# Filler products and an earlier first output product behind the experts' weights, with the first piece of w_out loaded last and decoded in halves

## The chip, the cores and the metric

The kernel runs on one core of one Trainium2 chip. The metric is the device time of one execution in microseconds (us), given as the median of three runs. One further execution was recorded by the profiler; all rows below are of that one.

## The reference

Attention over a window of 128 positions, then a soft mixture of experts, then a feed-forward layer with a leaky ReLU. The change lies between the last two.

```python
def _moe_ref(x, phi, w1, w2):                 # x 2304x512, 8 experts of 4 slots
    logits = x @ phi
    d = softmax over tokens of logits
    slot_input = (d.T @ x).reshape(E, S_per_e, D)
    for e in range(E):
        h = np.maximum(slot_input[e] @ w1[e], 0.0)
        slot_out[e] = h @ w2[e]
    c = softmax over slots of logits
    return c @ slot_out

def _moe2_ref(x, w_in, w_out):                # w_in 512x2048, w_out 2048x512
    h = x @ w_in
    g = np.maximum(0.01 * h, h)
    return g @ w_out
```

## The kernel before, in words

The program is one stream of instructions per engine, written out by hand: parts of the work are put into a list with a number each, the list is sorted by that number, and the instructions are issued in that order. Engines wait for one another through semaphores; within an engine nothing overtakes.

**The experts.** After attention, the experts' weights (units of 1 MB, four experts' blocks of 128 x 512 each) are multiplied as they arrive: 16 units of w1, then 16 units of w2 (line 824, numbered `i` = 0 to 15 by `g * FC + fc`). The last ten units have no room earlier and are loaded by line 793, each into a slot `p0`, `p1`, ... All these loads go through SP's queue, in the order of the program. Ahead of the last four units (`PRE`) SP also issues the first pieces of the next layer's weights: `load_wi(0)` and `load_wo(0)`, 1 MB each. After the last unit ScalarE copies the sum out of PSUM (line 859), TensorE transposes it (`to_soT`, line 762), and VectorE copies it into `soT` (line 765).

**The feed-forward layer.** c @ slot_out @ w_in is computed as c @ (slot_out @ w_in), so that a piece of w_in (256 columns, `NCH` = 8 pieces) is first multiplied with the 32 slots: `emit_M(c, 0)` (line 882, four products of 32 rows each), a copy by ScalarE (line 885), `emit_M(c, 1)` (line 887, one product that adds the four), a rounded copy by ScalarE (line 889) and the rest of the rounding by VectorE (line 890). Then follow units of 384 tokens x 128 columns: `stage1` (line 910), two activations by ScalarE (`round_g` line 914, `full_g` line 918), their difference by VectorE (`rest_g`, line 922), and `emit_o`, the output product: nine products of 512 columns (line 931), three for each of three groups of 128 tokens. Every two units of columns need a new piece of w_in and w_out. Both `emit_M` parts and `stage1` write one of two PSUM buffers named `ph`, so each waits until ScalarE has read the buffer written two before.

**Decoding.** w_in and w_out lie in memory as 64-bit floats. `decode` (line 719) turns a piece into 32-bit ones: two ScalarE activations on halves of 512 columns, and on VectorE two TENSOR_SCALAR and four SCALAR_TENSOR_TENSOR; a piece of w_out is then also split into a rounded part (a CAST by ScalarE) and a rest (a TENSOR_TENSOR by VectorE), again in halves. Half 0 of piece 0 of w_out holds the columns that units 0 and 1 use, half 1 those of units 2 and 3.

**The order.** Unit `n` has the number `n` for `stage1`, and `n + ZO["O"]` = `n + 3.986` for `emit_o`. Pieces are decoded, and `emit_M` issued, at numbers worked out from `YD[c]`:

```python
o = n + (ZO["O"] if n >= ZO["r"] else ZO["O"] - (ZO["r"] - n) * ZO["d"])
at_(-2, emit_M, 0, 0)
at_(-1 + ZO["M1"], emit_M, 0, 1)
for c in range(1, NCH):
    at_(YD[c] + ZO["M"], emit_M, c, 0)
    at_(YD[c] + ZO["M"] + ZO["m"], emit_M, c, 1)
```

So four `stage1`, both parts of `emit_M` for piece 0 and both for piece 1 stand ahead of the first output product. `warm` (line 150), in the attention part, multiplies the identity with itself into a buffer that nobody reads; each call of `matmul` there makes two records in the trace, since 32-bit products take two passes.

Of the kernel before, what the change touches and what calls it, by code (L numbers as in the profile page):

```python
# [9 lines left out]
F32 = mybir.dt.float32  # L10
# [11 lines left out]
def attn_softmoe_ffn(ctx: ExitStack, tc: tile.TileContext, q, k, v, phi, w1, w2, w_in, w_out, cst_in, out):  # L22
# [96 lines left out]
    with tc.manual_schedule():  # L119
# [552 lines left out]
        FPC = NF // NCH  # L672
        fw = DFF // NCH
        TB = 384
        x0 = off["x0"]

        def parts(w, *os):
# [110 lines left out]
        while i < len(units_w):  # L788
            if i == len(units_w) - PRE:
                load_wi(0, "p12")  # L790
                load_wo(0, "p13")
            o, src = put_w(i, j, slot(f"p{k}")[:, 0:512 * (4 - j)])
            nc.sync.dma_start(out=o, in_=src)  # L793
            i, j, k = i + 1, 0, k + 1
        csts = [t.bitcast(F32R).rearrange("p (t a s) -> p t a s", t=5, a=4) for t in (view("xT", 640, 512), ar[:, x0 + 1536:x0 + 2176])]
        cg = []

# [18 lines left out]

        for b in range(2):
            csplit(b)
        for g in range(E // 4):
            p2 = ps.tile([128, DM], F32, tag="pb0", name="pb")  # L820
            for fc in range(FC):
                t = W.pop((1, g, fc, 0))
                for j in range(4):
                    nc.tensor.matmul(p2[32 * j:32 * j + 32, :], lhsT=hT[g][:, fc, :], rhs=t[j],
                                     start=(fc == 0), stop=(fc == FC - 1), tile_position=(0, 32 * j))
                i = g * FC + fc
                if i == HI:
                    to_hT(1)
                if i == SOI:
                    to_soT(0)  # L830
                if i == 6:
                    load_wi(1, "a3")
                    cctx.close()
                    pools["b"] = ctx.enter_context(tc.tile_pool(name="bp", bufs=1, side="right", reuse_waits="tile"))
                    alloc_wo(0, "b0", "b1")
                    d0 = decode(0, False)
                    for f in d0[0] + d0[1]:
                        f()
                    d0 = decode(0, True)
                    load_wo(1, "a2")  # L840
                    load_wi(2, "b2")
                if i == 9:
                    for f in d0[0] + d0[1]:
                        f()
                if i == 1:
                    cg.extend(slot(x, F32R) for x in ("p11", "p10"))
                    ctr(0)
                    csplit(2)
                if i == 2:
                    ctr(1)  # L850
                    csplit(3)
                if i in (4, 5):
                    ctr(i - 2)
            if g == E // 4 - 1:
                load_wo(2, "p9")
                load_wi(3, "p0")
                load_wo(3, "p12")
            so = ar[:, x0 + F:x0 + F + DM]
            nc.scalar.copy(out=so, in_=p2)
            if g == E // 4 - 1:  # L860
                for f in d0[2][::2]:
                    f()
        to_soT(1)
        for f in d0[2][1::2]:
            f()
        bctx.close()


# [5 lines left out]
        rings["g1"], rings["g2"] = [[[gx[:, TB * i:TB * i + TB] for i in range(4)], 0] for gx in (cg[1], G2)]  # L874

        Mq = {}

        def emit_M(c, part):
            p = psc.tile([128, 512], F32, tag="ph", name="ph")
# [77 lines left out]
        def at_(y, f, *a):  # L957
            ev.append((y, len(ev), lambda: f(*a)))

        for n, u in enumerate(units):  # L960
            o = n + (ZO["O"] if n >= ZO["r"] else ZO["O"] - (ZO["r"] - n) * ZO["d"])
            at_(n, stage1, *u)
            at_(n + ZO["T"], round_g, *u)
            at_(n + ZO["H"], full_g, *u)
            at_(n + ZO["V"], rest_g, *u)
            at_(o, emit_o, *u)
            if u[2] == NF - 1 or (u[0], u[2]) == (0, FH - 1):
                for i in range(3):
                    at_(o + (.01 * i if u[0] in (0, 1, NB - 1) else i), finish)
        YD = {c: per * (c - 1) if 2 * c <= NCH else per * (NCH // 2 - 1) + 2 + 7 * (c - NCH // 2) for c in range(1, NCH + 1)}  # L970
        at_(-2, emit_M, 0, 0)
        at_(-1 + ZO["M1"], emit_M, 0, 1)
        for c in range(1, NCH):
            at_(YD[c] + ZO["M"], emit_M, c, 0)
            at_(YD[c] + ZO["M"] + ZO["m"], emit_M, c, 1)

        def dec(c, split, y, y1):
            ops = []

            def go(l, i):  # L980
                ops.extend(decode(c, split) if not ops else [])
                ops[l][i]()
            for i in range(2):
                at_(y + ZO["q"] + .01 * i, go, 0, i)
            for i in range(6):
                at_(max(y + ZO["D"] + ZO["w"] * i, y1), go, 1, i)
            for i in range(4 if split else 0):
                at_(y + ZO["t"] + ZO["u"] * (i // 2), go, 2, i)
        for c in range(1, NCH):
            if c == 1:  # L990
                dec(1, False, YD[c] - 2, ZO["f"])
            dec(c, True, YD[c], ZO["g"] if c == 1 else -9)
            if c + 1 < NCH:
                dec(c + 1, False, YD[c + 1] - 2, -9)
        at_(-.9, load_wi, 4, "p13")
        at_(2.05, load_wo, 4, "a3")
        sl = ("a2", "b2", "p9", "p0", "p12", "p13")
# [54 lines left out]
```

## Time and profile before

| | us |
|---|---|
| median of the three runs | 460.52 |
| lowest and highest of the three | 457.16, 460.90 |
| the profiled execution | 457.5 |
| its span, first to last instruction | 455.7 |

The profiled execution lies 0.3 us above the lowest run and 3.0 us below the median. In the page and the views times count from the start of the span. PE is TensorE, PEld its weight loads, DVE is VectorE, ACT is ScalarE, SP the queue that issues the DMAs; PEclk or the granted clock is the share of TensorE's full clock. A record's duration includes the time in which a product drains; records of one engine overlap, so the pace of a series is read from the distance of the starts or from the chain, not from one record's duration.

### The profile page before, as it was taken

The numbers are of one execution on the slowest core, as the hardware profiler recorded it, in microseconds if no ns is written. First come the engines' busy times: TensorE is split into PE (matmuls) and PEld (weight loads), VectorE is DVE, ScalarE is ACT, GpSimd is POOL, SyncE is SP. The second block draws the span as 40 slices with busy tenths as digits, with TensorE's granted clock in tenths as the row PEclk, the third lists the DMA queues.
The fourth block names the chain that finished last, engine by engine and source line by source line (L and its number), as shares of the span: only waits on it lengthen the run. The fifth ranks groups of instructions, "written<-read, shape, count | busy, mean of one in ns | idle before, by whom it ended". The sixth has DMA issues, their size and how long they took to land.

```text
span 455.7 us, 9878 instructions
## 1 busy us (share of the span) xinstructions
PE 432.9 (95%) x3506; PEld 338.9 (74%) x3506; DVE 278.3 (61%) x891; ACT 242.3 (53%) x560; POOL 109.8 (24%) x288
## 2 busy tenths in 40 slices
PE   7899999999999989996699999999999999999996
PEld 6797887888788764341277787787888888888885
DVE  5999999999999833033799857756223225224221
ACT  5576776777677531240677665556345333333331
POOL 3476676667477523020000000000000000000000
PEclk9999999999999999998589999999999999999999
DMA  9339778668669899999997300000003003001001
GB/s 170 97 118 231 211 219 232 170 200 238 179 199 239 261 337 340 371 391 388 399 384 251 116 1 0 1 1 0 1 0 138 1 0 140 1 1 47 23 1 69
DMA packets 66593, 70.30 MB, mean 154 GB/s; under 512 B 23056, under 2 KB 41648, under 8 KB 66544
## 3 DMA queue, kind: packets, MB, share of 16 engines
q1 hardware_dynamic: 66544, 69.66, 48.3%
q8 instruction: 28, 0.46, 0.4%
q14 instruction: 21, 0.17, 0.1%
HBM read 64.85 MB, written 4.72 MB: 153 GB/s over the span
## 4 chain that ended last, share of the span: by engine, by line
PE 83%; DMA 5%; DVE 4%; ACT 3%; SPq 2%; issue 1%; POOL 1%; ACTq 0%; DVEq 0%; POOLq 0%
PE acc L931 44%; PE o_ps L389 7%; PE sm L295 5%; PE ph L910 4%; PE st L336 4%; PE st L337 3%; PE tp L255 3%; DMA p<-in_moe_w_dram 3%; PE pb L773 3%; SPq L793 2%; PE tp L430 2%; ACT kb L268 1%; DVE junk L305 1%; PE ph L882 1%; PE tp L456 1%
## 5 line engine op out<-in xcount | busy, mean ns | idle before, releaser
L931 PE MATMUL acc<-p,p 128*128 128x512 f32 x648 | 161.0, 393 | 0.0
L931 PEld LDWEIGHTS acc<-p,p 128*128 128x128 f32 x648 | 120.4, 188 | 25.8 <-issue 1.2
L922 DVE TENSOR_TENSOR p<-ar,p 128x384 fp32r<-128x384 f32 x96 | 53.5, 557 | 103.9 <-ACT ar L918 103.6
L914 ACT ACTIVATE p<-ph 128x384 fp32r<-128x384 f32 x96 | 47.2, 492 | 107.1 <-PE ph L910 107.1
L931 PE MATMUL acc<-b,p 128*128 128x512 f32 x216 | 56.1, 404 | 0.0
L305 DVE CUSTOM_DVE_ANT_0 junk<-sm,ar 128x256 bf16<-128x256 f32 (+2 forms) x160 | 53.6, 375 | 3.2 <-PE sm L295 2.8
L931 PEld LDWEIGHTS acc<-b,p 128*128 128x128 f32 x216 | 40.9, 192 | 9.9 <-issue 1.2
L918 ACT ACTIVATE ar<-ph 128x384 f32<-128x384 f32 x96 | 46.6, 486 | 0.0
L344 ACT ACTIVATE ar<-st 128x512 f32<-128x512 f32 x64 | 38.3, 598 | 14.8 <-PE st L337 9.3
L389 PE MATMUL o_ps<-ar 128*64 128x65 f32 x1024 | 40.2, 225 | 0.7 <-POOL ar L360 0.7
L389 PEld LDWEIGHTS o_ps<-ar 128*64 128x64 f32 x1024 | 36.0, 138 | 5.1 <-issue 1.5
L336 PE MATMUL st<-kq 128*128 128x256 f32 (+1 forms) x160 | 39.8, 278 | 0.0
L295 PE MATMUL sm<-kb,qb 96*128 96x256 f32 (+2 forms) x160 | 35.0, 312 | 4.3 <-ACT kb L268 1.9
L337 PE MATMUL st<-qb,kb 128*128 128x256 f32 (+1 forms) x160 | 35.6, 269 | 0.7 <-DMA qb<-ms 0.7
L910 PE MATMUL ph<-p,p 128*128 128x384 f32 x96 | 33.1, 346 | 1.8 <-DVE p L890 0.9
L268 ACT ACTIVATE qb<-tp 64x288 fp32r<-64x288 f32 x64 | 27.7, 432 | 9.3 <-PE tp L255 7.8
L273 DVE SCALAR_TENSOR_TENSOR kq<-tp,qb 64x288 fp32r<-64x288 f32 x64 | 29.2, 457 | 4.2 <-ACT qb L268 2.2
L268 ACT ACTIVATE kb<-tp 64x288 fp32r<-64x288 f32 x64 | 27.9, 436 | 6.2 <-PE tp L255 4.9
L275 DVE TENSOR_TENSOR kq<-tp,kb 64x288 fp32r<-64x288 f32 x64 | 29.1, 455 | 1.7
L281 POOL TENSOR_SCALAR_AFFINE_SELECT kq<-qb 64x576 fp32r<-64x576 f32 x32 | 21.3, 664 | 35.2 <-ACT qb L268 30.0
L336 PEld LDWEIGHTS st<-kq 128*128 128x128 f32 (+1 forms) x160 | 28.6, 179 | 1.4 <-issue 0.9
L337 PEld LDWEIGHTS st<-qb,kb 128*128 128x128 f32 (+1 forms) x160 | 28.6, 179 | 0.9 <-DMA qb<-ms 0.9
(164 smaller groups left out, 575.7 us busy)
## 6 DMA issues: line engine op xcount, KB each, us to landing
p<-in_moe_w_dram SPq DMA_DIRECT2D x56, 256.0 KB
p<-in_moe_w_dram SPq DMA_DIRECT2D x9, 1024.0 KB
p<-in_moe_w_in_dram SPq DMA_DIRECT2D x5, 1024.0 KB
p<-in_moe_w_out_dram SPq DMA_DIRECT2D x5, 1024.0 KB
ar<-in_k_dram SPq DMA_DIRECT2D x32, 144.0 KB
ar<-in_q_dram SPq DMA_DIRECT2D x32, 144.0 KB
out_dram<-ar SPq DMA_DIRECT2D x18, 256.0 KB
ar<-in_v_dram SPq DMA_DIRECT2D x32, 128.0 KB
```

What stands on the lines that cost most here:

```text
L268: nc.scalar.activation(out=b1, in_=pr, func=AF.Copy, scale=2.0 ** (g % H - 2) if half else 1.0)
L295: nc.tensor.matmul(sl, lhsT=Q1[0:MROW, 128 * t:128 * t + mr], rhs=K1[0:MROW, c0:c1], start=True, stop=True)
L305: nc.vector.tensor_tensor_reduce(out=jk[0:mr, 0:n], in0=sl, in1=maskt[0:mr, m0:m0 + n], op0=ALU.add, op1=ALU.max, accum_out=mn[g % 2][0:mr ...
L336: nc.tensor.matmul(sl, lhsT=KX[:, k0:k1], rhs=QA[:, q0:q1], start=True, stop=False)
L337: nc.tensor.matmul(sl, lhsT=kb[g % R][:, k0:k1], rhs=qb[g % R][:, q0:q1], start=False, stop=True)
L344: nc.scalar.activation(out=e, in_=sts.pop((g, s)), func=AF.Exp, scale=2.0 ** -(g % H + 1))
L389: nc.tensor.matmul(o_ps[64 * u:64 * u + 64, t, :], lhsT=lt, rhs=r, start=st, stop=sp, tile_position=(0, 64 * u))
L910: nc.tensor.matmul(p, lhsT=mst[:, 128 * f:128 * f + 128], rhs=rhs, start=True, stop=True)
L914: nc.scalar.activation(out=G[t0, f][0], in_=H1[t0, f], func=AF.Prelu, alpha=0.01)
L918: nc.scalar.activation(out=gg, in_=H1.pop((t0, f)), func=AF.Prelu, alpha=0.01)
L922: nc.vector.tensor_tensor(out=g2, in0=G0.pop((t0, f)), in1=g1.bitcast(F32), op=ALU.subtract)
L931: nc.tensor.matmul(acc[t0][t], lhsT=(g1, g1, g2)[k][:, 128 * t:128 * t + 128], rhs=(WO1, WO2, WO1)[k][c][:, i], start=((f == 0 or (j, f) = ...
```

## The change

The load of piece 0 of w_out moves from ahead of the last four expert units to behind them. Its decoding, which was written into the experts' loop, moves into the list and is issued in halves, by numbers written out in a table `FIRST`, as are the decodings of piece 1. `keep` multiplies the identity with itself: 2, 8 and 8 times ahead of expert units 13, 14 and 15, then 4, 3, 3, 4 and 5 times between the steps that lead to the first output product (table `WX`). The last copy out of PSUM is shared by ScalarE and VectorE. Output products are issued closer to their `stage1` at first (`n + 1.9`, growing by 0.13 a unit up to the old distance), and `emit_M` for piece 1 behind the second output product.

```diff
+        WX = {13: 2, 14: 8, 15: 8, "s": 4, "t": 3, "m": 3, "b": 4, "h": 5}
...
             if i == len(units_w) - PRE:
                 load_wi(0, "p12")
-                load_wo(0, "p13")
...
             i, j, k = i + 1, 0, k + 1
+        load_wo(0, "p13")
...
+        wps = ps.tile([128, 128], F32, tag="w", name="w", bufs=1)
+
+        def keep(n, t):
+            for i in range(n):
+                nc.tensor.matmul(t[:, 0:128], lhsT=ident, rhs=ident, start=True, stop=True)
+
         for g in range(E // 4):
             p2 = ps.tile([128, DM], F32, tag="pb0", name="pb")
             for fc in range(FC):
                 t = W.pop((1, g, fc, 0))
+                keep(WX.get(g * FC + fc, 0), wps)
...
                     d0 = decode(0, False)
                     for f in d0[0] + d0[1]:
                         f()
-                    d0 = decode(0, True)
                     load_wo(1, "a2")
                     load_wi(2, "b2")
-                if i == 9:
-                    for f in d0[0] + d0[1]:
-                        f()
...
             so = ar[:, x0 + F:x0 + F + DM]
-            nc.scalar.copy(out=so, in_=p2)
             if g == E // 4 - 1:
-                for f in d0[2][::2]:
-                    f()
+                nc.scalar.copy(out=so[:, 0:256], in_=p2[:, 0:256])
+                nc.vector.tensor_copy(so[:, 256:512], p2[:, 256:512])
+                keep(WX["s"], wps)
+            else:
+                nc.scalar.copy(out=so, in_=p2)
         to_soT(1)
-        for f in d0[2][1::2]:
-            f()
+        keep(WX["t"], wps)
...
+        wpc = psc.tile([128, DM], F32, tag="acc5", name="acc", bufs=1)
...
-            o = n + (ZO["O"] if n >= ZO["r"] else ZO["O"] - (ZO["r"] - n) * ZO["d"])
-            at_(n, stage1, *u)
+            o = n + min(1.9 + .13 * n, ZO["O"])
+            y = n + (.2 if n >= 4 else 0)
+            at_(y, stage1, *u)
...
         at_(-2, emit_M, 0, 0)
+        at_(-1.9, keep, WX["m"], wpc)
         at_(-1 + ZO["M1"], emit_M, 0, 1)
-        for c in range(1, NCH):
+        at_(-.9, keep, WX["b"], wpc)
+        at_(1.05, keep, WX["h"], wpc)
+        at_(3.05, emit_M, 1, 0)
+        at_(3.5, emit_M, 1, 1)
+        for c in range(2, NCH):
...
+        FIRST = {(0, True): ((-2.5, -1.5), (-2.4, -.95, -2.3, -.94, -2.2, .38), (-.93, -.92, 1.18, 1.38)),
...
+        dec(0, True, 0, 0)
...
-                dec(c + 1, False, YD[c + 1] - 2, -9)
+                dec(c + 1, False, YD[c + 1] - 2, 3.5 if c == 1 else -9)
```

In SP's queue, where the last expert units and the first pieces are issued, stands before:

```order
L692 DMA p_3538<-in_moe_w_in_dram 128x4x512
L697 DMA p_3540<-in_moe_w_out_dram 128x2x1024
L793 DMA p_3542<-in_moe_w_dram 128x4x512
L793 DMA p_3544<-in_moe_w_dram 128x4x512
L793 DMA p_3546<-in_moe_w_dram 128x4x512
L793 DMA p_3548<-in_moe_w_dram 128x4x512
```

and now, with `load_wi` and `load_wo` one line further down in the file:

```order
L693 DMA p_3538<-in_moe_w_in_dram 128x4x512
L793 DMA p_3540<-in_moe_w_dram 128x4x512
L793 DMA p_3542<-in_moe_w_dram 128x4x512
L793 DMA p_3544<-in_moe_w_dram 128x4x512
L793 DMA p_3546<-in_moe_w_dram 128x4x512
L698 DMA p_3548<-in_moe_w_out_dram 128x2x1024
```

The four expert units move up by one load, and the piece of w_out stands behind them; all that follows keeps its place.

On TensorE, from expert unit 14 (before) and the fillers ahead of unit 15 (now) to the first output product (`pb` is the experts' sum, `w` and `acc` on the left of `ident` are what the fillers write, `ph` the shared buffer, `acc<-b` an output product), stands before:

```order
L824 MATMUL pb<-p_3546,ar 32x512 x4
L824 MATMUL pb<-p_3548,ar 32x512 x4
L762 MATMUL pa<-ident,ar 128x128 x4
L882 MATMUL ph<-ar 32x256 x4
L887 MATMUL ph<-ar,blk 128x256
L910 MATMUL ph<-p_3567,p_3749 128x384 x2
L882 MATMUL ph<-ar 32x256 x4
L910 MATMUL ph<-p_3567,p_3749 128x384
L887 MATMUL ph<-ar,blk 128x256
L910 MATMUL ph<-p_3567,p_3749 128x384
L931 MATMUL acc<-b_3657,p_3568 128x512 x3
```

and now, where line 824 is the filler and 832 the experts' product:

```order
L824 MATMUL w<-ident 128x128 x8
L832 MATMUL pb<-p_3546,ar 32x512 x4
L824 MATMUL w<-ident 128x128 x4
L763 MATMUL pa<-ident,ar 128x128 x4
L824 MATMUL w<-ident 128x128 x3
L888 MATMUL ph<-ar 32x256 x4
L824 MATMUL acc<-ident 128x128 x3
L893 MATMUL ph<-ar,blk 128x256
L824 MATMUL acc<-ident 128x128 x4
L916 MATMUL ph<-p_3568,p_3764 128x384 x2
L824 MATMUL acc<-ident 128x128 x5
L937 MATMUL acc<-b_3658,p_3569 128x512 x3
```

The second `emit_M` (both parts) and two of the four `stage1` have left the place ahead of the first output product, and 19 fillers stand there. Where they went, behind the first output product, is this:

```order
L916 MATMUL ph<-p_3568,p_3764 128x384 x2
L937 MATMUL acc<-b_3658,p_3569 128x512 x3
L937 MATMUL acc<-b_3659,p_3569 128x512 x3
L937 MATMUL acc<-b_3658,p_3765 128x512 x3
L888 MATMUL ph<-ar 32x256 x4
L893 MATMUL ph<-ar,blk 128x256
L937 MATMUL acc<-b_3658,p_3569 128x512 x3
```

The two parts of `emit_M` for piece 1 now follow each other with nothing between.

On ScalarE, from the last activations of the first two units to the second rounded copy, stands now (line 720 is `decode`, 920 and 924 the activations of a unit, 891 and 895 the copies of `emit_M`):

```order
L720 CAST b_3658<-ar 128x512
L720 ACTIVATE ar<-ar 128x512 x2
L920 ACTIVATE p_3569<-ph 128x384
L924 ACTIVATE ar<-ph 128x384
L720 ACTIVATE ar<-ar 128x512 x2
L720 ACTIVATE ar<-b_3669 128x512 x2
L891 COPY ar<-ph 128x256
L920 ACTIVATE p_3569<-ph 128x384
L924 ACTIVATE ar<-ph 128x384
L895 CAST p_3764<-ph 128x256
```

and before, from the second unit's activations on:

```order
L914 ACTIVATE p_3568<-ph 128x384
L918 ACTIVATE ar<-ph 128x384
L885 COPY ar<-ph 128x256
L914 ACTIVATE p_3568<-ph 128x384
L918 ACTIVATE ar<-ph 128x384
L889 CAST p_3749<-ph 128x256
```

Ahead of the copy of piece 1's first product now stand six activations of `decode` and one of its casts.

## Rows read from the trace of the kernel before

**Rows 1.** The page: busy shares, and granted clock in 40 slices.

```profile
PE 432.9 (95%) x3506; PEld 338.9 (74%) x3506; DVE 278.3 (61%) x891; ACT 242.3 (53%) x560; POOL 109.8 (24%) x288
...
PEclk9999999999999999998589999999999999999999
```

**Rows 2.** Windows: busy us (records) by engine, granted clock, DMA share, GB/s.

```profile
211.00:212.00 1.00, 0.00 (x0) 0.00 (x0) 0.00 (x0) 0.00 (x0) 0.00 (x0) 1.00 1.03 381
...
213.00:214.00 1.00, 0.17 (x4) 0.00 (x0) 0.00 (x0) 0.00 (x0) 0.00 (x0) 0.89 1.05 385
...
225.00:230.00 5.00, 4.08 (x15) 2.30 (x8) 4.94 (x11) 4.49 (x11) 0.00 (x0) 0.50 1.03 398
...
235.00:240.00 5.00, 5.00 (x23) 4.15 (x24) 4.94 (x12) 3.10 (x8) 0.00 (x0) 1.00 0.98 359
```

**Rows 3.** Timeline of PE: start, us, line, tiles, records, idle before.

```profile
209.40 1.06 PE L824 MATMUL pb<-p,ar 128*32 128x512 f32 x8 [0.28 <-DMA p<-in_moe_w_dram]
...
214.80 1.94 PE L824 MATMUL pb<-p,ar 128*32 128x512 f32 x8 [1.63 <-DMA p<-in_moe_w_dram]
...
228.75 3.21 PE L931 MATMUL acc<-b,p 128*128 128x512 f32 x9
...
262.65 2.23 PE L931 MATMUL acc<-p,p 128*128 128x512 f32 x9
```

**Rows 4.** Chain that ended last, in order of time: start, us, line, records.

```profile
171.28 0.86 PE o_ps L150 x6
...
179.06 8.72 PE pb L773 x80
187.78 1.02 PE pa L753 x8
...
228.95 3.01 PE acc L931 x9
231.96 0.17 PE ph L910
...
234.41 0.57 PE ph L882 x8
...
237.44 0.43 PE ph L887 x2
...
240.13 2.10 PE acc L931 x9
...
303.54 2.07 PE acc L931 x9
```

**Rows 5.** Timeline of DVE, columns as in rows 3.

```profile
205.25 0.75 DVE L719 TENSOR_SCALAR ar<-p 128x512 int32<-128x512 int32 x2
...
218.65 0.42 DVE L765 COPY ar<-pa 128x16 f32<-128x16 f32 x4 [9.92 <-PE pa L762]
...
229.78 0.76 DVE L719 TENSOR_SCALAR ar<-b 128x512 int32<-128x512 int32 x2
230.45 1.29 DVE L719 SCALAR_TENSOR_TENSOR ar<-b,ar 128x512 int32<-128x512 int32 x2
231.66 0.68 DVE L719 TENSOR_TENSOR b<-ar,b 128x512 fp32r<-128x512 f32 x1
...
248.92 0.43 DVE L890 TENSOR_TENSOR p<-ph,p 64x256 fp32r<-64x256 f32 x1 [0.47 <-ACT p L889]
```

**Rows 6.** Timeline of ACT, columns as in rows 3.

```profile
228.19 0.37 ACT L889 CAST p<-ph 128x256 fp32r<-128x256 f32 x1
228.46 1.25 ACT L719 ACTIVATE ar<-b 128x512 f32<-128x512 f32 x2
229.61 0.61 ACT L719 CAST b<-ar 128x512 fp32r<-128x512 f32 x1
230.12 0.48 ACT L914 ACTIVATE p<-ph 128x384 fp32r<-128x384 f32 x1
230.51 0.48 ACT L918 ACTIVATE ar<-ph 128x384 f32<-128x384 f32 x1
```

More of the change, by code (lines that the diff above doesn't have):

```diff
@@ L960, in attn_softmoe_ffn @@
         for n, u in enumerate(units):
-            o = n + (ZO["O"] if n >= ZO["r"] else ZO["O"] - (ZO["r"] - n) * ZO["d"])
-            at_(n, stage1, *u)
-            at_(n + ZO["T"], round_g, *u)
-            at_(n + ZO["H"], full_g, *u)
-            at_(n + ZO["V"], rest_g, *u)
+            o = n + min(1.9 + .13 * n, ZO["O"])
+            y = n + (.2 if n >= 4 else 0)
+            at_(y, stage1, *u)
+            at_(y + ZO["T"], round_g, *u)
+            at_(y + ZO["H"], full_g, *u)
+            at_(y + ZO["V"], rest_g, *u)
             at_(o, emit_o, *u)
@@ L971, in attn_softmoe_ffn @@
         at_(-2, emit_M, 0, 0)
+        at_(-1.9, keep, WX["m"], wpc)
         at_(-1 + ZO["M1"], emit_M, 0, 1)
-        for c in range(1, NCH):
+        at_(-.9, keep, WX["b"], wpc)
[3 more added lines that the diff above has]
+        for c in range(2, NCH):
             at_(YD[c] + ZO["M"], emit_M, c, 0)
             at_(YD[c] + ZO["M"] + ZO["m"], emit_M, c, 1)
+        FIRST = {(0, True): ((-2.5, -1.5), (-2.4, -.95, -2.3, -.94, -2.2, .38), (-.93, -.92, 1.18, 1.38)),
+                 (1, False): ((1.2, 1.21), (.385, .386, .39, .391, 1.4, 1.41), ()),
+                 (1, True): ((2.25, 2.26), (1.6, 1.61, 2.4, 2.41, 3.4, 3.41), (3.6, 4.6, 3.61, 4.61))}
         def dec(c, split, y, y1):
             ops = []
+            if (c, split) in FIRST:
+                for l, xs_ in enumerate(FIRST[c, split]):
+                    for i, x in enumerate(xs_):
+                        at_(x, lambda l, i: (ops.extend(decode(c, split) if not ops else []), ops[l][i]()), l, i)
+                return
             def go(l, i):
```

## The prediction

> **What bounds the kernel now.** I read the page first: TensorE is busy 95% of the span, and its granted clock is at full level in all but two of the 40 slices [rows 1]. So I looked for the place where TensorE is neither busy nor fast. The windows show it: at 211 to 212 us TensorE does nothing while the DMA engines are full (1.03) at 381 GB/s, and at 213 to 214 the granted clock begins to fall [rows 2]. From 225 to 230 it is at 0.50, which is the level of 1.2 GHz; from 235 to 240 it is back at 1.00, the level of 2.4 GHz [rows 2]. The timeline of TensorE gives the cause: expert units 13 and 15 wait for their DMA, and the first output product starts at 228.75, though unit 15 started at 214.80 [rows 3]. In the chain the first output product takes 3.01 us, a later one 2.10 [rows 4]. The rows of VectorE and ScalarE in that stretch tell what else is full: VectorE is busy 4.94 of 5 us from 225 to 230 and again from 235 to 240, ScalarE 4.49 and 3.10 [rows 2]. After 228 VectorE's first wait of some length is 0.47 us at 248.92 [rows 5].
>
> **The end point of the sum.** From the 14th output product on, at 262.65 [rows 3], both orders have issued the same products, and the rest is one product after another on TensorE. So the change is worth what it moves that one start. Each engine's instructions are laid out below in the new order, each starting when its engine is free and its data are there.
>
> **Unit prices.** Eight records of an expert unit: 8.72 for 80 records, 0.87 a unit [rows 4]. One output product: nine records in 2.08, between the rows of 2.10 and 2.07 [rows 4]. `stage1` 0.17, and one `emit_M` pair 0.57 + 0.43 = 1.00 [rows 4]. ScalarE, by the distance of starts: two decode activations 229.61 - 228.46 = 1.15, a cast 0.51, an activation of a unit 0.39, an `emit_M` copy 0.27 [rows 6]. VectorE: two TENSOR_SCALAR 0.67, two SCALAR_TENSOR_TENSOR 1.21 [rows 5].
> A filler is not in the trace with these neighbours. `warm` made six records in 0.86, 0.143 each, and eight records of the same width on the identity take 1.02, 0.128 each [rows 4]. Two records a filler give 0.26 by the nearer row and 0.29 by the other. I take 0.26, and as the low end 0.22, about as far below it as 0.29 is above.
> The Trainium skill speaks of this price ("TensorE: Matmul & The Clock Gate", back-to-back issue gap): pairs of weight load and 128-column product in a stream come about 81 ns apart. By that a filler would be an estimated 0.16 and the 18 fillers ahead of unit 15 would cost 1.8 us less, the sum then 456.8. The rows above, which are 32-bit products on the same engine, say 0.128, and they decide.
>
> **Step 1, the load moved.** The DMA engines are full here, and units 13 and 15 start 5.40 us apart with two loads of 1 MB between [rows 3], so a load is 2.70. With w_out's first piece behind them, units 13, 14 and 15 land about at 206.7, 209.4 and 212.1, and w_out's piece at 214.8. All later loads keep their place in the queue. Piece 4 of w_in takes w_out's slot and must now wait for the decode, to about 222; loads still queued cover that.
>
> **Step 2, the fillers.** TensorE is idle for 0.28 ahead of unit 13, so unit 12's last record ends at 209.12 [rows 3]; 0.19 of that is drain (1.06 - 0.87), and the next can start at 208.93. Then 2 fillers 0.52, unit 13 0.87, 8 fillers 2.08, unit 14 0.87, 8 fillers 2.08: unit 15 starts at 215.35. Its weights came 3.3 us before that. So the earlier landing is spent on fillers, and unit 15 starts 0.55 later than before. The clock should stay at 2.4 GHz, since TensorE now has no idle us like that at 211.
>
> **Step 3, the way to the first output product.** With unit 15 over at 216.22, the fillers follow one another with the steps between them: 4 fillers 1.04, transposes 0.51, 3 fillers 0.78, `emit_M` 0.57, 3 fillers 0.78, 0.43, 4 fillers 1.04, two `stage1` 0.34, 5 fillers 1.30: the first output product at 223.05, with a few hundredths of waiting. ScalarE's and VectorE's copies lie beside the fillers. That is 5.70 ahead of 228.75 [rows 3]. On this way decode has its first half done at 219.9 on VectorE and the second at 224.0, both in time for the products that need them.
>
> **Step 4, what is pushed behind it.** Two `stage1` and an `emit_M` pair, 0.34 + 1.00 = 1.34, now stand behind the first output product. Against that the first output product runs at the full clock: 3.01 - 2.08 = 0.93 less.
>
> **Step 5, the waits that replace the old one.** The decode of w_out's first piece, on VectorE 0.67 + 2 x 1.21 = 3.09, used to lie at 205.25, where VectorE stood idle afterwards until 218.65 (9.92 of idle) [rows 5]. It now lies behind 218, where VectorE is full. Laid out in the new order, ScalarE has its second cast of that piece at 224.06; then 0.51, decode of w_in's piece 1 1.15, two activations 0.78, decode of w_out's piece 1 1.15, of w_in's piece 2 1.15, the `emit_M` copy 0.27, two activations 0.78: 229.85. Only then are the PSUM buffer and the copy there for the second part of `emit_M`, which follows its first part directly. TensorE was ready at 228.49 and goes on at 229.98: 1.49. In the same way ScalarE delays later `emit_M` parts and `stage1` by 2.29 in sum, and VectorE, which is busy without a break from 221 to 251, delays `emit_M` of pieces 1 and 2 by 0.78, `stage1` by 0.12, and the 6th and 8th output product by 0.83 and 0.55. All waits up to the 14th: 6.06. Before, the same stretch has 0.70 (33.90 between the two starts, less 13 x 2.08 + 13 x 0.17 + 3 x 1.00 + 0.93 = 33.18).
>
> **The sum.** -5.70 + 1.34 - 0.93 + (6.06 - 0.70) = +0.07. Laid out by the same prices, the old order reaches the 14th output product 1.1 too early, so I add 1.1 for what such a layout misses: +1.1 or so against the profiled execution, 457.5 + 1.1 = 458.6. Its time lies 3.0 below the median of the runs, and nothing in one trace says where these 3.0 lie; by the median it would be 461.6. Now that the last units no longer wait for their DMA, some of that spread may go, so I take 459.5, nearer to the profiled one.
>
> Ends: with fillers at 0.22 and nothing added, 1.5 (37 fillers x 0.04) and 1.1 less, 456.0; with fillers at 0.29, 37 x 0.03 = 1.1 more, 459.7 by the profiled execution and 462.7 by the median.
>
> **Rivals.**
> *The engines keep up.* The waits of step 5 fall away, since ScalarE and VectorE have shares of 53% and 61% over the span [rows 1]. Then 5.36 comes off: 453.2 by the profiled execution. By the profiled execution it is faster by over 1% once half of them, 2.7, is gone. Against it: VectorE is at 4.94 of 5 in the very stretch [rows 2] and 3.09 is added. Chance 0.10.
> *The clock is not held.* The fillers are too thin for it, the clock falls near 214 as before and comes back near 231. Each step on the way to the first output product then takes up to twice its price, fillers too, and the decode work stands behind it as well: laid out like this the first output product starts at 230.0 in place of 223.05, and the 14th 6.6 us later than in the forecast: 465.2, and by the median 468.2. It decides from the point where the clock stays low past about 227. For it: it fell with units of 0.87 in 2.70 us; against it: `warm` held it in the tail of attention, where its records stand [rows 1, 4]. Chance 0.10.
> *The clock falls later.* In step 5 TensorE has 1.00 of work between 227.6 and 230.4, not much more than the stretch before the fall at 213 to 214 [rows 2]. If it falls there and comes back near 236, 1.2 is added: 459.8, by the median 462.8. Chance 0.25.
> *The moved load gains nothing.* This is in the forecast: the earlier landing is spent on fillers.
>
> **How the numbers follow.** About 1%, 4.6 us, is what a measurement of this kernel tells from no change. Forecast 0.55; with the clock falling later, which also ends within 1%, 0.80. Faster 0.10, same 0.80, slower 0.10. The range takes in both ends and the later fall: 456.0 to 463.5.
>
> **What would show it.** Right: the clock at 1.00 through 210 to 226; unit 15 near 215.3 without a wait for DMA; the first output product near 223; a gap of about 1.5 us ahead of the second part of piece 1's `emit_M`, released by ScalarE; VectorE without a break from 221 to about 250; the 14th output product between 262 and 264. Wrong: a first output product past 226, a clock of 0.50 before it, or the 14th output product before 260.

## The result: 0.6% slower, and the profile after

| | before | after |
|---|---|---|
| median of 20 runs each | 458.06 us (455.0 to 461.99) | 460.77 us (458.68 to 463.56) |
| profiled execution, its span | 457.5 us, 455.7 | 461.09 us, 459.3 |
| mean granted clock of the profiled execution | 0.981 | 0.995 |

The ratio after to before is 1.0063, with an interval of 1.004 to 1.0085. The change makes the kernel a little slower, by more than the measurement's uncertainty. The 20 runs of before have a median 2.5 us under that of the three runs shown ahead of the prediction (460.52).

The page of after, engines and granted clock, answers to [rows 1]:

```profile
PE 440.2 (96%) x3580; PEld 345.3 (75%) x3580; DVE 278.9 (61%) x892; ACT 242.5 (53%) x560; POOL 109.3 (24%) x288
...
PEclk9999999999999998999999999999999999999999
```

The two low slices of before are gone. There is a new one, the 16th, which lies around 178 us, ahead of everything that the change touches. The windows of after show both (columns as in [rows 2]):

```profile
178.00:179.00 1.00, 1.00 (x8) 0.15 (x7) 0.49 (x2) 0.42 (x2) 0.00 (x0) 0.72 1.06 389
179.00:181.00 2.00, 2.00 (x13) 0.29 (x5) 0.52 (x2) 0.00 (x0) 0.00 (x0) 0.50 0.47 155
181.00:182.00 1.00, 1.00 (x7) 0.64 (x10) 0.32 (x2) 0.00 (x0) 0.00 (x0) 0.58 0.92 324
...
210.00:226.00 16.00, 15.91 (x131) 10.77 (x123) 4.83 (x16) 3.90 (x9) 0.00 (x0) 1.00 1.04 394
```

From 210 to 226 the clock is at 1.00 and TensorE is busy 15.91 of 16 us: the fillers do what they say. From 179 to 181 it is at 0.50.

The timeline of TensorE in after, over the stretch of [rows 3]. L824 is the filler, L832 an expert unit, L763 the transposes ahead of its copies, L937 an output product, L888 and L893 the two parts of `emit_M`:

```profile
209.24 0.66 PE L763 MATMUL pa<-ident,ar 128*128 128x128 f32 x4
...
213.32 2.05 PE L824 MATMUL w<-ident 128*128 128x128 f32 x16
215.30 1.06 PE L832 MATMUL pb<-p,ar 128*32 128x512 f32 x8
216.29 2.05 PE L824 MATMUL w<-ident 128*128 128x128 f32 x16
218.28 1.06 PE L832 MATMUL pb<-p,ar 128*32 128x512 f32 x8
...
225.98 2.34 PE L937 MATMUL acc<-b,p 128*128 128x512 f32 x9
...
228.51 2.26 PE L937 MATMUL acc<-b,p 128*128 128x512 f32 x9
231.00 1.13 PE L888 MATMUL ph<-ar 128*32 128x256 f32 x8 [0.23 <-ACT ar L720]
232.60 0.70 PE L893 MATMUL ph<-ar,blk 128*128 128x256 f32 x2 [0.47 <-ACT ar L891]
232.95 2.46 PE L937 MATMUL acc<-b,p 128*128 128x512 f32 x9
...
266.25 2.23 PE L937 MATMUL acc<-p,p 128*128 128x512 f32 x9
...
279.88 0.64 PE L888 MATMUL ph<-ar 128*32 128x256 f32 x8
```

Two rows of before stand against the first and the last of these:

```profile
206.61 0.66 PE L762 MATMUL pa<-ident,ar 128*128 128x128 f32 x4
...
276.28 0.64 PE L882 MATMUL ph<-ar 128*32 128x256 f32 x8
```

The first line is the one to measure from: these transposes start at 206.61 in before and at 209.24 here, so everything in this stretch is 2.63 later for reasons that lie ahead of it. With 2.63 taken off, unit 15 (218.28) starts at 215.65, the first output product at 223.35, the 14th (266.25) at 263.62. In [rows 3] they stand at 214.80, 228.75 and 262.65. So the first output product comes 5.40 us earlier, and 13 products later the kernel is 0.97 us late.

**Where the 5.40 went.** The chain of after from 223 to 250, its shares by line:

```profile
by line: DVE ar L720 50.7%; issue 17.3%; DVE p L928 12.5%; DVE b L720 8.5%; DVE p L896 4.8%; PE acc L937 1.9%; PE ph L893 1.8%; ACT p L895 1.4%; DVEq L720 0.5%; DVEq L928 0.4%; PE acc L824 0.4%; DVE p L720 0.3%
```

TensorE's output products (L937) hold 1.9% of it, ScalarE's copy (L895) 1.4%. VectorE holds 77%: its decode (L720) 59%, the differences of the units (L928) 12.5%, the corrections of `emit_M` (L896) 4.8%. A further 17.3% is time in which the engine of the chain waited for nothing that the profile shows. VectorE's timeline in after, to be read beside [rows 5], shows when that work can begin and when it is over:

```profile
219.87 0.42 DVE L865 COPY ar<-pb 128x256 f32<-128x256 f32 x1 [9.52 <-ACT ar L864]
...
221.24 0.42 DVE L720 TENSOR_SCALAR ar<-p 128x512 int32<-128x512 int32 x1
221.69 0.69 DVE L720 SCALAR_TENSOR_TENSOR ar<-p,ar 128x512 int32<-128x512 int32 x1
222.47 0.69 DVE L720 SCALAR_TENSOR_TENSOR ar<-ar 128x512 int32<-128x512 int32 x1
224.01 0.43 DVE L896 TENSOR_TENSOR p<-ph,p 64x256 fp32r<-64x256 f32 x1 [0.85 <-ACT p L895]
...
254.20 0.43 DVE L896 TENSOR_TENSOR p<-ph,p 64x256 fp32r<-64x256 f32 x1
255.58 0.56 DVE L928 TENSOR_TENSOR p<-ar,p 128x384 fp32r<-128x384 f32 x1 [0.96 <-ACT ar L924]
```

VectorE waits 9.52 us until the experts are over (219.87), then the new decode of `w_out`'s first piece begins (221.24), and from 224.01 it has no wait until 255.58. The line at 254.20, the correction of piece 3, answers to the one at 248.92 in [rows 5]: with 2.63 off it is 251.57, 2.65 later than before. TensorE was brought to its output products early, and then had to wait, mostly for an engine whose stretch of full work starts only when the experts end. That stretch now also holds the 3.09 us of moved decode; experiment 8 shows how much of them counts.

### The profile page after: what moved, and what is told of

It reads as the page before. It is cut to its first block, busy times and chain, and to the rows that moved or that the text cites. A ratio compares the mean times of both kernels' runs of the same rounds, so it can differ in the third digit from the quotient of the medians.

```text
span 459.3 us, 10006 instructions
## 1 busy us (share of the span) xinstructions
PE 440.2 (96%) x3580; PEld 345.3 (75%) x3580; DVE 278.9 (61%) x892; ACT 242.5 (53%) x560; POOL 109.3 (24%) x288
## 4 chain that ended last, share of the span: by engine, by line
PE 84%; DVE 9%; issue 2%; ACT 2%; DMA 2%; SPq 0%; POOL 0%; DVEq 0%; ACTq 0%
PE acc L937 40%; PE o_ps L389 7%; PE sm L295 5%; PE st L336 4%; PE st L337 3%; PE pb L774 3%; PE pb L832 3%; PE ph L916 3%; PE tp L255 3%; DVE ar L720 3%; PE tp L430 2%; PE w L824 1%; DVE junk L305 1%; DVE kq L273 1%; PE tp L456 1%
## 5 line engine op out<-in xcount | busy, mean ns | idle before, releaser
L937 PE MATMUL acc<-p,p 128*128 128x512 f32 x648 | 161.1, 393 | 0.0
L937 PEld LDWEIGHTS acc<-p,p 128*128 128x128 f32 x648 | 120.4, 188 | 25.4 <-issue 0.8
L928 DVE TENSOR_TENSOR p<-ar,p 128x384 fp32r<-128x384 f32 x96 | 53.5, 557 | 106.5 <-ACT ar L924 106.3
L937 PE MATMUL acc<-b,p 128*128 128x512 f32 x216 | 55.5, 399 | 0.6 <-DVE p L928 0.6
L937 PEld LDWEIGHTS acc<-b,p 128*128 128x128 f32 x216 | 40.0, 188 | 10.1 <-DVE p L928 1.4
```

The lines of the kernel that those rows point to most:

```text
L928: nc.vector.tensor_tensor(out=g2, in0=G0.pop((t0, f)), in1=g1.bitcast(F32), op=ALU.subtract)
L937: nc.tensor.matmul(acc[t0][t], lhsT=(g1, g1, g2)[k][:, 128 * t:128 * t + 128], rhs=(WO1, WO2, WO1)[k][c][:, i], start=((f == 0 or (j, f) = ...
```

## The experiments

The following table cuts each profile at two lines of TensorE's timeline: the transposes ahead of unit 11 (209.24 above) and the first line of piece 5's `emit_M` (279.88 above). From there to the end of the span it is 179.4 to 179.5 us in every one of them. "Stage" is the time between the two lines, which holds all that the change touches. "Unit 15" is the start of the last expert unit after the transposes, "behind it" the rest of the stage from there. Each row is one execution; before_2 to before_4 and after_2 are the repeats at the end of this section. Where the units run without a gap, the start of unit 15 is estimated as four fifths of their series, and stands with "about".

| kernel | transposes | unit 15 | first output product | stage | behind it |
|---|---|---|---|---|---|
| before | 206.61 | 8.19 | 228.75 | 69.67 | 61.48 |
| before_2 | 213.59 | 7.20 | 234.76 | 69.02 | 61.82 |
| before_3 | 209.17 | 9.20 | 232.33 | 71.41 | 62.21 |
| before_4 | 206.64 | 7.25 | 227.85 | 68.82 | 61.57 |
| after | 209.24 | 9.04 | 225.98 | 70.64 | 61.60 |
| after_2 | 208.39 | 9.03 | 225.13 | 70.59 | 61.56 |
| before, 8 fillers ahead of the experts | 211.62 | 7.17 | 231.02 | 67.72 | 60.55 |
| after, the same | 209.49 | 9.03 | 226.23 | 70.61 | 61.58 |
| after without unit fillers | 207.83 | about 4.1 | 219.56 | 65.60 | about 61.5 |
| before with fillers in its waits | 206.87 | 7.36 | 226.19 | 66.47 | 59.11 |
| after without any filler | 209.97 | about 4.1 | 221.26 | 66.47 | about 62.3 |
| after with few fillers | 208.08 | 5.49 | 220.60 | 66.86 | 61.37 |
| after, old spacing of products | 207.47 | 9.04 | 229.96 | 71.32 | 62.28 |
| after, old load and decode | 209.71 | 9.03 | 226.46 | 69.75 | 60.72 |

The last column is the main finding. Behind the start of unit 15 the changed kernel takes 61.60 and 61.56, the kernel before 61.48 to 62.21: the early first output product gains nothing there. What differs is when unit 15 starts. Of the 0.97 between the first profiles of the two, 0.85 lies ahead of that start (9.04 against 8.19), where the unit fillers stand.

**1 and 2. Is a delay ahead of the experts taken in by before's waits for DMA?** Eight fillers ahead of the first expert unit, in each kernel:

```diff
+        pd = ps.tile([128, 128], F32, tag="w", name="w", bufs=1)
+        for i in range(8):
+            nc.tensor.matmul(pd, lhsT=ident, rhs=ident, start=True, stop=True)
```

> The kernel before, with 8 fillers (about 2.0 us of TensorE) put ahead of the experts' first products; the output is the same. Theory A (the old order has 3.6 us of waiting for DMA at expert units 13 to 15, which swallows whatever makes TensorE late ahead of it): the time stays within 0.7 us of before, ratio 0.9985 to 1.0015, and the waits at units 13 to 15 shrink by 2.0. Theory B (a delay ahead of the experts simply adds, in both orders): 2.0 us slower, ratio 1.0044.

> The changed kernel with the same 8 fillers ahead of the experts' first products. Theory A (the changed order has fillers where the wait for DMA was, so nothing swallows a delay): 2.0 us slower than the changed kernel, ratio to before 1.0105 to 1.011. Theory B also 2.0 slower; only with the run on the kernel before the two part. If the changed order had slack left: ratio 1.006 to 1.008.

Measured: before with the delay 460.75 us, 1.0034 (1.0014 to 1.0055); after with it 461.48 us, 1.0063 (1.004 to 1.0085), both against before. Before gets slower: theory B's 1.0044 lies in the interval, and theory A's range, which ends at 1.0015, only touches its edge. TensorE's timeline of before with the delay:

```profile
211.62 0.66 PE L765 MATMUL pa<-ident,ar 128*128 128x128 f32 x4
212.20 2.78 PE L827 MATMUL pb<-p,ar 128*32 128x512 f32 x24
216.08 1.07 PE L827 MATMUL pb<-p,ar 128*32 128x512 f32 x8 [1.10 <-DMA p<-in_moe_w_dram]
218.79 1.07 PE L827 MATMUL pb<-p,ar 128*32 128x512 f32 x8 [1.64 <-DMA p<-in_moe_w_dram]
```

The transposes are 5.01 later than in the profile of before (2.0 by the fillers, 8 x 0.248, the rest lies ahead of them). The waits of 1.10 and 1.64 are still there, 2.74 in place of the 3.56 in the profile of before (0.28, 1.65 and 1.63), and not 2.0 less as theory A had it. So the loads came later as well, which would fit with their slots being released by TensorE's first units; that was not shown. The stage is 1.95 shorter, but unit 15 starts 7.17 after the transposes, about as in two of the four profiles of before (7.20 and 7.25), which have no delay. So this one profile does not show that the delay was taken in.

After with the delay lands where after landed without it, not at its expected 1.0105. It lies in the range that the expectation gave for slack left in the new order, but its stage is 70.61, as without the delay, so the slack is not there. The fillers stand at the place where after's clock fell; its windows now show none of it there:

```profile
172.00:184.00 12.00, 11.67 (x107) 6.99 (x109) 4.01 (x17) 1.53 (x8) 3.74 (x10) 1.00 0.82 289
```

Six of its eight runs have a mean clock of 0.999 or 1.0, and their mean is 461.38. The seven such runs of after have 459.39. Between these the delay adds 1.99, which is its whole price (8 x 0.248 = 1.98): by this sorting the new order swallows nothing, and the medians hide it, since seven of 20 runs of after and six of eight here are at such a clock.

**3. Are the fillers between the units needed?** Only their counts go:

```diff
-        WX = {13: 2, 14: 8, 15: 8, "s": 4, "t": 3, "m": 3, "b": 4, "h": 5}
+        WX = {"s": 4, "t": 3, "m": 3, "b": 4, "h": 5}
```

> The changed kernel without the 18 fillers ahead of expert units 13, 14 and 15; those behind unit 15 stay. Theory A (these fillers spend the earlier landing of the weights, and keep TensorE without slack): unit 15 starts on its landing, about 3 us earlier against the experts' products than in the changed kernel, the clock stays at 1.00 as only 1.4 us is idle ahead of it, and the time is 2.5 to 3.5 us below the changed kernel, ratio to before 0.9985 to 1.001. Rival C (the clock needs them): the clock falls to 0.50 between unit 15 and the first output product, and the time is that of the changed kernel or more, ratio 1.006 to 1.012.

Measured: 456.53 us, 0.9949 (0.9926 to 0.9971), under both kernels by more than the intervals. Theory A had the direction, and the gain is larger than it expected. TensorE's timeline of this kernel:

```profile
207.83 0.66 PE L763 MATMUL pa<-ident,ar 128*128 128x128 f32 x4
208.42 4.50 PE L832 MATMUL pb<-p,ar 128*32 128x512 f32 x40
212.85 1.16 PE L824 MATMUL w<-ident 128*128 128x128 f32 x8
...
219.56 2.35 PE L937 MATMUL acc<-b,p 128*128 128x512 f32 x9
```

The last five units run as one series of 40 records, with no wait for DMA. The experts end 5.0 us earlier after the transposes (212.85 against 219.27 in after, less 207.83 and 209.24), and the stage is 5.04 shorter: the whole of it stays, unlike the 5.40 of the first output product. It is more than the price of 18 fillers, 18 x 0.248 = 4.46, since the units now also run without gaps. That fits the reading of the VectorE timeline above. What brings the end of the experts forward also brings VectorE's stretch forward; what only brings the output products forward hardly does (experiment 7).

**4. Before with fillers in its DMA waits.** Its order and its loads stay; fillers stand ahead of units 14 and 15 and among the steps up to the first `stage1`, by calls of `keep` as in the changed kernel:

```diff
+        WX = {14: 6, 15: 6, "s": 2, "t": 1, "m": 1, "b": 3}
...
```

> The kernel before with fillers alone: 6 ahead of units 14 and 15 (1.5 of the 1.65 us that TensorE waits there), 2, 1, 1 and 3 between the steps that follow; loads, decoding and order as before. Theory A: the clock stays at 1.00 from 209 to 240, the 14th output product starts 1.7 us earlier, ratio 0.996 to 0.998 (a part is lost as less delay is swallowed). Rival D (fillers as such make the changed kernel slower): ratio 1.002 to 1.006.

Measured: 458.04 us, 0.9989 (0.996 to 1.0017). This is inconclusive: the expected 0.996 to 0.998 and no change both lie in the interval. In its profile the clock still falls, from 224 to 230 (0.72 in the mean), where theory A had it at 1.00 up to 240. Unit 15, here without a wait, and the stage:

```profile
214.23 1.06 PE L832 MATMUL pb<-p,ar 128*32 128x512 f32 x8
...
273.34 0.64 PE L893 MATMUL ph<-ar 128*32 128x256 f32 x8
```

Behind unit 15 it takes 59.11, 2.37 less than before, the shortest in the table. So in the old order a clock that stays up longer may be worth over 2 us. But this profile is of the shortest of its 12 runs (454.56), and the median shows no such gain; why is open.

**5 and 6. No filler, and few.** First all counts 0, then only the steps' fillers at 2, 1, 1, 2, 0:

```diff
-        WX = {13: 2, 14: 8, 15: 8, "s": 4, "t": 3, "m": 3, "b": 4, "h": 5}
+        WX = {"s": 0, "t": 0, "m": 0, "b": 0, "h": 0}
```

> The changed kernel without any filler (37 fewer than the changed kernel, 19 fewer than the one without those ahead of the units). Theory A (only the fillers behind unit 15 are needed to hold the clock, and a part of them stands in the way): the clock falls to 0.50 between unit 15 and the third output product, the way to the first output product grows, ratio to before 0.998 to 1.004. Rival C2 (no filler is needed, as TensorE no longer waits for the units): the clock stays, 0.6 us below the run without unit fillers, ratio 0.992 to 0.995.

> The changed kernel without the 18 unit fillers and with 6 in place of 19 behind unit 15 (2, 1, 1, 2 and none). Theory A: the clock stays, TensorE follows ScalarE and VectorE more closely and the first output product starts 1 to 1.3 us earlier than with 19, but VectorE and ScalarE, full in the stretch that follows, give back half: ratio 0.992 to 0.995. Rival C: the clock falls, ratio 0.998 to 1.004.

Measured: no filler 456.42 us, 0.9934 (0.9899 to 0.9968); few 457.5 us, 0.9972 (0.9937 to 1.0007), which is not told apart from its neighbours: the ranges of both its theories reach into the interval. In the profile with few fillers the clock stays at 1.00, and unit 15 waits for its load, which experiments 3 and 5 do not show:

```profile
213.57 1.06 PE L832 MATMUL pb<-p,ar 128*32 128x512 f32 x8 [1.26 <-DMA p<-in_moe_w_dram]
```

The window of the kernel without fillers:

```profile
219.00:226.00 7.00, 5.82 (x15) 4.37 (x15) 6.42 (x13) 4.52 (x10) 0.00 (x0) 0.55 1.03 396
```

The clock does fall (0.55), as theory A had it, and yet the time is the one that rival C2 gave for a clock that stays. The stage is 66.47, against 65.60 in experiment 3, where the fillers among the steps hold the clock: 0.87 for the fall, less what these 19 fillers cost themselves. VectorE is busy 6.42 of these 7 us. In the new order, where VectorE is the limit of this stretch, holding TensorE's clock with fillers buys less than a microsecond.

**7. Does closing the first output products pay?** The old distances of the products, and `emit_M` and decode of piece 1 in their old places; all fillers stay. This kernel computes other values than the reference; the reason is not known here, presumably the decode buffers are used in another order. It has as many records as after on TensorE (3580), VectorE (892) and ScalarE (560), and serves for its time alone.

```diff
-            o = n + min(1.9 + .13 * n, ZO["O"])
-            y = n + (.2 if n >= 4 else 0)
+            o = n + ZO["O"]
+            y = n
...
-        at_(3.05, emit_M, 1, 0)
-        at_(3.5, emit_M, 1, 1)
-        for c in range(2, NCH):
+        for c in range(1, NCH):
...
```

> The changed kernel with all its fillers, but with output products as far behind their stage1 as in the kernel before, emit_M for piece 1 and the decoding of piece 1 in their old places. Theory A (the earlier first output product is given back as waits for ScalarE and VectorE within the next 13): within 0.8 us of the changed kernel, ratio 1.004 to 1.008, the first output product about 5 us later and the 14th within 1 us. Rival E (the close output products are the gain in the change, spent on fillers): 3 to 5 us slower than the changed kernel, ratio 1.012 to 1.017.

Measured: 461.65 us, 1.0064 (1.003 to 1.0098), as theory A had it. Its timeline of TensorE:

```profile
207.47 0.66 PE L763 MATMUL pa<-ident,ar 128*128 128x128 f32 x4
...
228.90 0.70 PE L893 MATMUL ph<-ar,blk 128*128 128x256 f32 x2 [1.00 <-ACT ar L891]
229.96 2.27 PE L937 MATMUL acc<-b,p 128*128 128x512 f32 x9
```

Its first output product comes 22.49 after the transposes, in after 16.74: 5.75 earlier. The time of the two kernels is not told apart by their intervals, and the stages differ by 0.68: of 5.75 at the first output product 0.68 is left at the end of the stage.

**8. What does moving `w_out`'s load and decode cost?** Load and first decode back in their old places; all fillers stay:

```diff
                 load_wi(0, "p12")
+                load_wo(0, "p13")
...
-        load_wo(0, "p13")
...
```

> The changed kernel with all its fillers, but with the first piece of w_out loaded ahead of the last four expert units and its main decoding among the experts' products, as in the kernel before. Theory A (3.1 us of VectorE and 1.1 of ScalarE then leave the full stretch): 0.5 to 1.2 us below the changed kernel, ratio 1.003 to 1.0055, from fewer waits between the second and the ninth output product; unit 15 starts where it does in the changed kernel, as the fillers and not the landing set it. Rival F (the load's place decides, units land later): 2 us or more above the changed kernel, ratio 1.010 or more.

Measured: 460.16 us, 1.0033 (1.0002 to 1.0065), within what theory A gave, though its interval overlaps that of after. Two lines of its TensorE timeline:

```profile
209.71 0.66 PE L763 MATMUL pa<-ident,ar 128*128 128x128 f32 x4
...
218.74 1.07 PE L832 MATMUL pb<-p,ar 128*32 128x512 f32 x8
```

Unit 15 starts 9.03 after the transposes, in after 9.04 (218.28 - 209.24). With the fillers there, the earlier landing gains nothing. The stage is 0.89 shorter, far less than the 3.09 of decode that lie outside VectorE's stretch again. The groups of VectorE from 220 to 256, two of after and then the same two of this kernel (the last figures are the idle time ahead of the group), show where the rest goes:

```profile
L928 DVE TENSOR_TENSOR p<-ar,p 128x384 fp32r<-128x384 f32 x11 | 6.1, 552 | 1.0 <-ACT ar L924 1.0
L896 DVE TENSOR_TENSOR p<-ph,p 64x256 fp32r<-64x256 f32 x4 | 1.7, 428 | 0.9 <-ACT p L895 0.8
...
L932 DVE TENSOR_TENSOR p<-ar,p 128x384 fp32r<-128x384 f32 x11 | 6.1, 556 | 1.6 <-ACT ar L928 1.6
L900 DVE TENSOR_TENSOR p<-ph,p 64x256 fp32r<-64x256 f32 x4 | 1.7, 428 | 2.8 <-ACT p L899 2.7
```

VectorE is idle for 4.4 in place of 1.9: some 2.5 of the work taken out turn into waiting for ScalarE at the start of the stretch, after which VectorE has no wait from 226.35 to 255.19. So the moved decode is a small part of what holds the stage; the larger part is the work that VectorE had there already.

**9 to 12. Single executions: how much of the difference is the execution?** Three more of before, unchanged, and one more of after:

> The kernel before once more, for its trace. In the trace of before, TensorE is late by nothing ahead of the units that wait for DMA. Theory A2 (the clock falls in many executions for some 3 us around the start of the experts, at 168 to 182; the old order's 3.6 us of waiting at units 13 to 15 takes that in, the changed order has none): where the clock falls there, the waits at units 13 to 15 are shorter by about 1.5 and the stretch from the copy-out transposes ahead of unit 11 to piece 5's emit_M is 68.0 to 68.7 in place of 69.67. Theory B2 (landing follows TensorE, nothing is taken in): 69.5 to 69.9.

> As before_2: by theory A2 the stretch is 68.0 to 68.7 if the clock falls ahead of the experts' unit 11, by theory B2 69.5 to 69.9; without such a fall both say 69.3 to 70.0.

> As before_2: by theory A2 the stretch is 68.0 to 68.7 if the clock falls ahead of the experts' unit 11, by theory B2 69.5 to 69.9; without such a fall both say 69.3 to 70.0.

> The changed kernel once more. Both theories: the stretch from the copy-out transposes ahead of unit 11 to piece 5's emit_M is 70.5 to 70.8, as in its first trace and with the delay put ahead, whatever the clock did before, as no wait for DMA is left in it.

Measured: before 463.85, 461.84 and 456.7 us, after 460.21. The stage of after is 70.59, beside 70.64 and 70.61 above: it repeats. The stages of before are 69.02, 71.41 and 68.82. Windows of the first of these repeats:

```profile
41.00:44.00 3.00, 3.00 (x18) 3.00 (x17) 0.00 (x1) 1.54 (x4) 0.00 (x0) 0.50 1.00 248
172.00:180.00 8.00, 7.39 (x40) 5.31 (x40) 2.46 (x9) 1.63 (x8) 2.45 (x7) 0.57 1.04 386
```

With a fall of the clock shortly ahead of the experts (0.57) the stage is 69.02, between the two theories; without one there it is 71.41 and 68.82, outside what both gave. So these executions decide nothing on whether before takes such a fall in. They do show where before's spread in the stage comes from. Unit 15 in before_2, before_3, before_4 and after_2, in this order:

```profile
220.79 1.94 PE L824 MATMUL pb<-p,ar 128*32 128x512 f32 x8 [1.62 <-DMA p<-in_moe_w_dram]
...
218.37 1.94 PE L824 MATMUL pb<-p,ar 128*32 128x512 f32 x8 [0.75 <-DMA p<-in_moe_w_dram]
...
213.89 1.94 PE L824 MATMUL pb<-p,ar 128*32 128x512 f32 x8 [2.57 <-DMA p<-in_moe_w_dram]
...
217.42 1.07 PE L832 MATMUL pb<-p,ar 128*32 128x512 f32 x8
```

In before it starts when its load lands, 7.20 to 9.20 after the transposes, and the stage follows it. In after it starts behind its fillers, at 9.03 and 9.04, with no wait for DMA.

## Why the prediction failed, point by point

**Step 1, the load moved: as predicted in what it gives.** Without the unit fillers, units 11 to 15 run with no wait (experiments 3 and 5); in experiment 6 unit 15 waits for its load and starts 5.49 after the transposes, just where the prediction had its landing (212.1 - 206.61). I wrote that the earlier landing is spent on fillers; with the old load the start of unit 15 does not move (experiment 8).

**Step 2, the fillers: right.** From one start to the next, 16 records take 1.98 (215.30 - 213.32), 0.248 a filler against my 0.26. This decides against the estimate of 0.16 that I had worked out from the Trainium skill ("TensorE: Matmul & The Clock Gate", back-to-back issue gap). Unit 15 stands at 215.65, predicted 215.35.

**Step 3, the first output product: right**, 223.35 for 223.05. The rival by which the clock is not held falls: 1.00 from 210 to 226.

**Steps 4 and 5: right in size, not in whose the waits are.** The second part of piece 1's `emit_M` starts at 232.60, or 229.97 with 2.63 off, where I had 229.98, and ScalarE releases it. Between the starts of the second and third output product lie 4.44 us (228.51 to 232.95), 1.36 more than a product and an `emit_M` pair. VectorE is full for 30 us as expected. Up to the 14th output product the waits come to 6.68 (40.27 between the two starts, less 13 products, 15 `stage1` and 4 `emit_M` pairs at my prices), where I had 6.06. But I gave 3.78 of them to ScalarE (1.49 + 2.29). Of the 2.2 that TensorE's rows show as waits from 223 to 256, ScalarE ends 1.0 and VectorE 1.2, and the chain from 223 to 250 gives 1.4% to ScalarE and 77% to VectorE. The rival by which the engines keep up falls with it. The rival by which the clock falls a second time in this stretch does not happen: it is at 1.00 from 206 to 280 in after, in after_2 and in after with the delay.

**The sum: right in its corrected form, with some luck.** The change gives +0.97 in the stage, and I had +0.07 by the layout and 1.1 for what the layout misses. Of that 1.1, 0.30 lay on the way to the first output product (-5.40 for -5.70) and 0.62 in the waits. The luck is in the execution that was profiled: its unit 15 started at 8.19, between the extremes. Against the other three stages of before the same stage of after would be 1.6 and 1.8 longer or 0.8 shorter.

**The step that failed is the last, the placing of this sum**: "Now that the last units no longer wait for their DMA, some of that spread may go, so I take 459.5, nearer to the profiled one." It put the forecast under the 460.52 shown, as a small gain, though the sum said a loss. Two things were wrong with it.

First, the median of three runs that I measured the spread from was itself high: 20 runs give 458.06, so most of the 3.0 above the profiled execution was not there to go. On that base the sum gives 458.06 + 1.1 = 459.2, 1.6 short of the measured 460.77.

Second, the spread of the units' waits did go, but at its long end. The four profiles of before have unit 15 at 7.20 to 9.20 and a stage of 68.82 to 71.41; after has it behind the fillers at 9.03 and 9.04, later than three of the four, and behind it nothing is gained. So less spread meant a longer stage, not a shorter one: in the mean of the profiles 70.62 for 69.73. The shortest of the 20 runs rose from 455.0 to 458.68, the longest from 461.99 to 463.56.

Another part of the spread goes with the mean granted clock of each run. I sorted the runs by it; those of before were taken with the experiments, not with the 20 runs of after:

| | runs | mean time |
|---|---|---|
| before (all runs beside the experiments), clock 0.981 or higher | 42 of 63 | 458.22 |
| before, clock lower | 21 of 63 | 460.49 |
| after, clock 0.999 or 1.0 | 7 of 20 | 459.39 |
| after, clock lower | 13 of 20 | 461.53 |

0.981 is the mean clock of the profile of before, whose falls are the two slices of [rows 1]. Such a mean does not say where a fall lies, so the cut at 0.981 is a rough one: before with the delay has 0.985 in a profile that shows a further fall between 30 and 60 us (0.94). Between the upper rows the change costs 459.39 - 458.22 = 1.17, near the 0.97 of the stage and the 1.1 predicted. The lower runs cost some 2.2 more in both kernels and are 65% of after's and 33% of before's, which gives the rest of the difference of these means (460.78 - 458.98 = 1.80). Against the 20 runs of before that belong to the same measurement, whose mean is 458.38, the difference is 2.40, so 0.6 more is not accounted for.

A profile of before had such falls at 41 to 44 and 172 to 180, one of after at 178 to 182. In the profile of after, this fall (1.59 us) and an attention stage that was 1.04 later ahead of it account for the 2.63 by which the transposes start late.

**What stays open.** Of the 2.7 between the two medians the stage explains about 0.9. The rest lies ahead of the stage, and the sorting puts a part of it, 0.6, down to runs with a lower clock; its cause is open. Whether after has more such falls because of the change, or by the sample, was not shown; they lie ahead of the moved code. The profiles hint at the change: between 166 and 186 us the clock is under 1.00 in five of eight profiles of the new order (0.91 in the mean of that window, in after_2 too) and in one of six of the old. That before's waits for DMA take part of a fall in was argued and not shown: against it stands experiment 1, where the loads came later with the units; for it, that with 8 fillers in both kernels the medians differ by 0.73 only (461.48 - 460.75); and the single executions leave it undecided.

**A version that beats both** came out of this: the changed kernel without its 18 unit fillers (0.9949), or without any (0.9934). Their intervals overlap, and both gains are under 1%.

## What to carry to other kernels

A filler is free only in a wait; when the same change also takes the wait away, as the moved load did here, the fillers are plain work on the path, 4.46 us for 18 of them by their price and 5.04 in the stage. Before work is pulled forward on one engine, look for the next engine that is full in that stretch and for the event that its stretch starts from: moving that event forward shortened the stage by all of its 5.0 us, moving the first engine alone by 5.75 shortened it by 0.68. Where the last load lands varies from run to run, measure in more than one profile from that landing on, before a stage is said to be shorter. And a profiled execution or three runs are a weak base for a placing within 0.5%: sort the runs by granted clock first, and don't let a spread of unknown cause work for the forecast.

## What was unexpected of the hardware

The granted clock falls to 0.50 for some microseconds at places that change from one execution of a kernel to the next (before: 41 to 44 and 172 to 180 us in one of its profiles and not in the first; after: 178 to 182 in the first, 0.74 there in the second). The mean granted clock of a run sorts the 20 runs of after into three groups that do not overlap in time: seven with 0.999 or 1.0 take 458.68 to 459.74, seven with 0.995 or 0.996 take 459.76 to 461.32, six with 0.991 to 0.993 take 461.68 to 463.56. Eight fillers at one of these places went with a clock of 1.00 there and in six of eight runs a mean of 0.999 or 1.0. And with a fall in a stretch where VectorE is the limit, 0.55 over 7 us without fillers, the stage was 0.87 us longer than with 19 fillers that prevent it, and these bought no time that can be measured (456.53 with them, 456.42 without).
